# Taking the scale of tanh and exp from ScalarE registers in an attention loop

## The chip, the cores and the metric

The kernel runs on one core of a Trainium2 chip. The metric is the device time of one execution in microseconds (us). The kernel before was run three times; the median is 474.38 us (473.76 to 475.51). One further execution was profiled, and all rows below come from that one.

## The reference, cut to what matters

The program is an attention with soft-capped scores, followed by a mixture of experts in which every token goes to its best expert. In the attention there are 8 batches, 12 heads, 448 positions and a head size of 64, all in fp32:

```python
scale = 1.0 / np.sqrt(q.shape[-1])                      # 0.125
scores = scale * np.matmul(q, k.transpose(0, 1, 3, 2))
scores = cap * np.tanh(scores / cap)
scores = scores - np.max(scores, axis=-1, keepdims=True)
attn = np.exp(scores)
attn = attn / (np.sum(attn, axis=-1, keepdims=True) + 1e-09)
attn_out = np.matmul(attn, v)
...
expert_idx = np.argmax(x @ w_gate, axis=1)              # 3584 tokens, 8 experts, at most 80 kept in each
h = np.maximum(x[tok_idx] @ w1[e], 0.0)
out[tok_idx] = gate_w[tok_idx, None] * (h @ w2[e])
```

`cap` is an input of the program (30.0 here), so it is known only when the program runs.

## The kernel before

The attention is a loop over 24 units of work (`u`), each with four heads of one batch. A unit's score matrix is cut into 7 blocks of 128x896. For each block `scores` lets TensorE (PE) multiply q and k into a PSUM tile `sc`, of which there are two, and ScalarE (ACT) then writes `e = tanh(scl * sc)` to SBUF at line 1206, where `scl` is 0.125/cap. `expo` at line 1210 turns `e` in place into `exp(capt * e)`, in three pieces of 128x1792 (two blocks) and one of 128x896. So a unit has 7 tanh and 4 exp instructions, 11 in all, and the loop has 168 and 96. GpSimd (POOL) adds up parts of `e` for the row sums (lines 1216 and 1218), PE multiplies the `e` of the unit before with the values (`av`, lines 1237 and 1270) and with ones (`sp`), and VectorE (DVE) inverts the row sums (lines 1278 to 1283) and scales the result (`x`, line 1290).

The order of the instructions inside the loop is written out by hand in the string `STEPS`, under a manual schedule: `q` is a block of scores with its tanh, `e` an exp, `v` and `r` are passes of PE over the values of the unit before, `p` a sum on GpSimd, `s` and `n` the steps of VectorE. At the marks `b`, steps of the gate and of the routing of earlier batches are slipped in by a planner with estimated costs. Every engine runs its own instructions in that order. What stands ahead of the loop, from `scale()` on, is put in order by the scheduler of the kernel language, which goes by the order of the program and by what is ready.

`scl` and `capt` are SBUF columns of 128x1: `scale()` (lines 140 to 143) loads `cap` into `capt` by DMA, and VectorE makes `scl` of it. ScalarE reads one of these columns as the scale operand of each tanh and exp. In the first microseconds ScalarE's queue also issues two of the transfers of `load(0)` (line 1168): the lower halves of the first tiles of k and q. `guards()` (lines 195 to 203) has three small ACTIVATE instructions on `capt`, and one table load goes ahead of them.

After the loop the experts run from line 1609 on. Their weights are fetched by DMA at line 868 into a ring, of which eight buffers exist during the attention and ten more come from memory that the attention gives back at its end. At the very end, at line 1647, every engine loads one flag from SBUF into a register.

Of the kernel before, what the change touches and what calls it, by code (L numbers as in the profile page):

```python
# [9 lines left out]
I32 = mybir.dt.int32  # L10
AF = mybir.ActivationFunctionType
# [5 lines left out]
B, H, S, D = 8, 12, 448, 64  # L17
# [101 lines left out]
def attn_moe(ctx, tc, q2, k, v, cap, wg, w1, w2, capacity, ct, out):  # L119
    nc = tc.nc  # L120
# [11 lines left out]
    capt = consts.tile([128, 1], F32, name="capt")  # L132
    scl = consts.tile([128, 1], F32, name="scl")
# [6 lines left out]
    def scale():  # L140
        nc.sync.dma_start(capt, cap.broadcast_to([128, 1]))
        nc.vector.reciprocal(scl, capt)
        nc.vector.tensor_scalar(scl, scl, 0.125, None, op0=ALU.mult)
# [706 lines left out]
    wts, regs = [], {}  # L850
# [265 lines left out]
    st = {"laid": set(), "banks": ["misc"], "held": {}, "take": None, "read": 0, "late": False}  # L1116
# [29 lines left out]
    with ExitStack() as a2:  # L1146
# [8 lines left out]
        def load(u):  # L1155
            b, j = u // NQ, 2 * (u % NQ)
            qt = st["q", u] = qkp.tile([128, 2, S], F32, name=f"qt{u}", tag="qt")
            kt = st["k", u] = qkp.tile([128, 2, S], F32, name=f"kt{u}", tag="kt")
            parts = [(p, slice(0, 2), slice(0, S)) for p in (kt, qt)]
            if u == 0:  # L1160
                one, two, w0, w1 = slice(0, 1), slice(1, 2), slice(0, KR + CK), slice(KR + CK, S)
                parts = [(kt, one, w0), (qt, one, slice(0, S)), (kt, one, w1), (kt, two, slice(0, S)), (qt, two, slice(0, S))]
            for n, (p, x, y) in enumerate(parts):
                for h in range(2):
                    w = slice(64 * h, 64 * h + 64)
                    queue = nc.scalar if u == 0 and h == 1 and n < 2 else nc.sync
                    src = k[b, j + x.start:j + x.stop, :, h, y] if p is kt else q2[b, j + x.start:j + x.stop, w, h]
                    queue.dma_start(p[w, x, y], src.rearrange("j p s -> p j s"))
# [17 lines left out]
        def scores(u, x):  # L1186

            if ("e", u) not in st:
                st["e", u] = ep.tile([CK, 2 + 4 * NK, S], F32, name=f"e{u}", tag="e")
            ps = pss.tile([CK, 2, 512], F32, name=f"sc{u}_{x}", tag="sc")  # L1190
            if x == 0:
                for pr in range(2):
                    for m in range(4):
                        for h in range(2):
                            w = slice(64 * h, 64 * h + 64)
                            i, y = m // 2, NK * CK * (1 - h) + 32 * (m % 2)
                            nc.tensor.matmul(ps[32 * m:32 * m + 32, h, HQ * pr:HQ * pr + HQ], st["k", u][w, pr, y:y + 32], st["q", u][w, pr, HQ * i:HQ * i + HQ],
                                             start=True, stop=True)
            else:
                pr, c = divmod(x - 1, NK)  # L1200
                for m in range(4):
                    for h in range(2):
                        w = slice(64 * h, 64 * h + 64)
                        y = KR * h + c * CK + 32 * m
                        nc.tensor.matmul(ps[32 * m:32 * m + 32, h, :S], st["k", u][w, pr, y:y + 32], st["q", u][w, pr], start=True, stop=True)  # L1205
            nc.scalar.activation(st["e", u][:, 2 * x:2 * x + 2], ps[:, :, :S], AF.Tanh, scale=scl)  # L1206

        def expo(u, x0, x1):
            e = st["e", u][:, 2 * x0:2 * x1]
            nc.scalar.activation(e, e, AF.Exp, scale=capt)  # L1210

        def esum(u, pr, i):
            e = st["e", u][:, 2 + 2 * NK * pr:2 + 2 * NK * (pr + 1)]
# [261 lines left out]
        st["begun"] = 0  # L1475
        st["wait"] = lambda: (now.__setitem__(1, now[0]), ready_at.__setitem__(1, clock[1]))
        scale()
        load(0)
        ready = ps1.tile([128, 512], F32, name="ready", tag="sp")
        for _ in range(NSTART):  # L1480
# [21 lines left out]
        for w in range(NU + 1):  # L1502
# [13 lines left out]
            for i, x in enumerate(todo):  # L1516
                k_ = x[0]
                a_ = [int(y) for y in x[1:]]
                if k_ == 'q' and w < NU:
                    scores(w, TURNS[a_[0]])  # L1520
                elif k_ == 'q':
                    begin()
                elif k_ == 'e':
                    expo(w, *RUNS[a_[0]])
                elif k_ == 'p':
                    if w not in DIRECT:
# [166 lines left out]
```

## Time and profile before

| | us |
|---|---|
| median of three runs | 474.38 (473.76 to 475.51) |
| the profiled execution, its time | 474.13 |
| the profiled execution, its span | 472.3 |
| busy: PE / ACT / DVE / POOL | 437.2 / 331.9 / 244.4 / 239.7 |
| mean granted clock of TensorE | 0.986 of full speed |

The span runs from the first to the last instruction; 1.8 us of the execution lie outside it. A row of a group of instructions gives its line, engine, operation, the tiles written and read (out<-in), the shape, how often it occurs, its busy time, the mean of one in ns, and the idle time of the engine ahead of it with what ended it. The chain of work that ended last is followed back from the last instruction to what released it, or to the instruction before it on its engine. "PEld" is TensorE's loading of weights, "issue" is time in which the profile shows no wait. A queue's name with a q at its end (SPq, ACTq) stands for instructions that the engine's sequencer handles itself, such as the issue of a transfer or a load into a register.

### The profile page before, as it was taken

What the parts mean: (1) busy time and instruction counts of PE and PEld (TensorE: products, weight loads), DVE (VectorE), ACT (ScalarE), POOL (GpSimd) and SP (SyncE); (2) the same over time, 40 slices, a digit from 0 to 9 for tenths busy, and PEclk for the clock granted to TensorE, in tenths of its full rate; (3) what the DMA queues carried; (4) which work ended last, traced back from release to release, by engine and by line L of the source; (5) the groups of instructions that cost most, each with busy time, mean ns of one, the idle gap of its engine ahead of it and who ended that gap; (6) DMA issues with size and microseconds to landing.
All of it is one profiled execution on the core that took longest, in us unless ns stands there. A gap on an engine that the chain in (4) does not pass through costs nothing.

```text
span 472.3 us, 21423 instructions
## 1 busy us (share of the span) xinstructions
PE 437.2 (93%) x9533; PEld 224.0 (47%) x9533; DVE 244.4 (52%) x769; ACT 331.9 (70%) x349; POOL 239.7 (51%) x152
## 2 busy tenths in 40 slices
PE   7799989998999999899979999999799999999990
PEld 3344434444443444445434454443245667764670
DVE  2133355337535663775257856998537998510000
ACT  5999998998999899898969999979501221211210
POOL 1666655675765566665546755656425032372022
PEclk9999999999999999999989999999899999999997
DMA  6776694697679559745724672893727999999961
GB/s 159 162 193 196 181 281 131 177 266 195 197 191 265 141 162 267 200 145 157 213 63 130 177 198 79 244 232 104 237 71 270 399 333 327 338 393 408 398 256 30
DMA packets 68261, 101.10 MB, mean 214 GB/s; under 512 B 12448, under 2 KB 50608, under 8 KB 68160
## 3 DMA queue, kind: packets, MB, share of 16 engines
q1 hardware_dynamic: 66048, 96.23, 66.5%
q0 software_dynamic: 1920, 3.25, 2.1%
q8 instruction: 77, 1.26, 1.2%
q14 instruction: 24, 0.20, 0.1%
q10 hardware_dynamic: 192, 0.17, 0.1%
HBM read 76.11 MB, written 23.80 MB: 212 GB/s over the span
## 4 chain that ended last, share of the span: by engine, by line
PE 62%; ACT 14%; DVE 12%; DMA 6%; issue 4%; POOL 1%; SPq 0%; POOLq 0%; DVEq 0%
PE sc L1205 16%; PE av L1237 16%; PE hp L891 8%; ACT e L1206 8%; ACT e L1210 6%; DMA w<-in_w_dram 5%; PE yp L891 4%; PE sp L1237 3%; PE lgp L1316 2%; PE sp L1268 2%; DVE x L1290 2%; PE av L1270 2%; DVE w L319 2%; PE hp5a L891 1%; PE pd L447 1%
## 5 line engine op out<-in xcount | busy, mean ns | idle before, releaser
L1206 ACT ACTIVATE e<-sc,scl 128x896 f32<-128x896 f32 x168 | 164.1, 1002 | 21.2 <-PE sc L1205 21.1
L1237 PE MATMUL av<-e,vr 64*32 64x448 f32 x2304 | 163.4, 545 | 7.2 <-DVE x L1290 6.8
L1210 ACT ACTIVATE e<-e,capt 128x1792 f32<-128x1792 f32 (+1 forms) x96 | 153.5, 1599 | 0.8
L1205 PE MATMUL sc<-qt,kt 64*32 64x448 f32 x2304 | 141.2, 544 | 8.8 <-ACT e L1206 8.3
L1216 POOL TENSOR_TENSOR t<-e 128x896 f32<-128x896 f32 x46 | 96.9, 2107 | 90.6 <-ACT e L1210 90.1
L1218 POOL TENSOR_TENSOR t<-t,e 128x896 f32<-128x896 f32 x46 | 97.4, 2118 | 41.1 <-ACT e L1210 36.8
L1237 PEld LDWEIGHTS av<-e,vr 64*32 64x32 f32 x2304 | 53.4, 107 | 68.8 <-issue 42.2
L1205 PEld LDWEIGHTS sc<-qt,kt 64*32 64x32 f32 x2304 | 39.8, 106 | 56.5 <-issue 34.6
L1278 DVE STREAM_TRANSPOSE st<-sp 128x448 f32<-128x448 f32 x24 | 15.6, 650 | 91.0 <-PE sp L1237 84.8
L941 POOL DMA_INDIRECT out_dram<-ysv,si x18 | 18.6, 1035 | 61.2 <-ACT ysv L939 53.5
L1270 PE MATMUL av<-e,vr 64*32 64x224 f32 x384 | 46.5, 349 | 0.0
L891 PE MATMUL hp<-w,xt 128*32 128x256 f32 x720 | 42.4, 381 | 2.3 <-DVE xt L691 1.4
L1237 PE MATMUL sp<-t,ones 64*32 64x448 f32 x368 | 44.5, 543 | 0.0
L891 PE MATMUL yp<-w,thv 128*32 128x192 f32 x960 | 41.9, 327 | 0.6 <-DMA w<-in_w_dram 0.4
L1270 PE MATMUL av<-e,vx 64*32 64x224 f32 x384 | 41.7, 349 | 0.0
L1290 DVE TENSOR_TENSOR x<-av,r 128x448 f32<-128x448 f32 x48 | 27.7, 619 | 16.4 <-PE av L1237 16.3
L891 PEld LDWEIGHTS yp<-w,thv 128*32 128x32 f32 x960 | 30.1, 110 | 10.4 <-DMA w<-in_w_dram 2.4
L891 PEld LDWEIGHTS hp<-w,xt 128*32 128x32 f32 x720 | 21.9, 109 | 20.1 <-DMA w<-in_w_dram 3.4
L1270 PEld LDWEIGHTS av<-e,vr 64*32 64x32 f32 x384 | 22.6, 107 | 16.7 <-issue 15.9
L441 DVE TENSOR_SCALAR_CACHE_REDUCE gb<-krow,kc 112x896 bf16<-112x896 f32 (+7 forms) x36 | 30.0, 876 | 0.5 <-PE pd L447 0.5
L1268 PE MATMUL sp<-e,ones 64*32 64x224 f32 x384 | 27.9, 349 | 0.0
L1299 DVE STREAM_TRANSPOSE xb<-x 128x448 f32<-128x448 f32 x48 | 27.9, 619 | 0.0
(241 smaller groups left out, 417.4 us busy)
## 6 DMA issues: line engine op xcount, KB each, us to landing
w<-in_w_dram SPq DMA_DIRECT2D x36, 512.0 KB
w<-in_w_dram SPq DMA_DIRECT2D x48, 384.0 KB
vr<-in_v_dram SPq DMA_DIRECT2D x24, 512.0 KB
out_dram<-zero SPq DMA_DIRECT2D x14, 768.0 KB
xs<-xb SPq DMA_DIRECT2D x32, 336.0 KB
kt<-in_k_dram SPq DMA_DIRECT2D x46, 224.0 KB
qt<-in_q_dram SPq DMA_DIRECT2D x46, 224.0 KB
vx<-in_v_dram SPq DMA_DIRECT2D x48, 32.0 KB
```

The source lines that it names most:

```text
L441: nc.vector.tensor_scalar(g, krow[:, x:y], kp, 0.0, op0=ALU.is_ge, op1=ALU.add, accum_out=a)
L891: nc.tensor.matmul(spot(ps, g, q)[32 * j:32 * j + 32], of(g), w[:, q * j:q * j + q], start=(kk == 0 and g % 2 == 0), stop=(kk == last and ...
L1205: nc.tensor.matmul(ps[32 * m:32 * m + 32, h, :S], st["k", u][w, pr, y:y + 32], st["q", u][w, pr], start=True, stop=True)
L1206: nc.scalar.activation(st["e", u][:, 2 * x:2 * x + 2], ps[:, :, :S], AF.Tanh, scale=scl)
L1210: nc.scalar.activation(e, e, AF.Exp, scale=capt)
L1216: nc.gpsimd.tensor_tensor(t1, e[:, 0:2], e[:, 2:4], op=ALU.add)
L1218: nc.gpsimd.tensor_tensor(st["es", u, pr], st["es", u, pr], e[:, 4:6], op=ALU.add)
L1237: behind(nc.tensor.matmul(ps[32 * g:32 * g + 32, :S], v_, e, start=first, stop=final))
L1268: behind(nc.tensor.matmul(st["sp", u][32 * g:32 * g + 32, HQ * i:HQ * i + HQ], ones[w, 0:32], e, start=(part == 0), stop=False))
L1270: behind(nc.tensor.matmul(st["av", u, f][32 * g:32 * g + 32, HQ * i:HQ * i + HQ], last_of(u, pr, h, i)[w, 32 * f:32 * f + 32], e, start=Fa ...
L1290: nc.vector.tensor_tensor(st["x", u][:, f], st["av", u, f][:, :S], st["r", u], op=ALU.mult)
L1299: nc.vector.transpose(st["xt", b][:, :, j, :], st["x", u][:, f].rearrange("p (a b) -> p a b", b=32))
```

## The change

Two registers of ScalarE are allocated. Right after `scale()` and ahead of `load(0)` one is loaded from the first element of `scl` and the other from the first element of `capt`, as raw 32-bit values. Every tanh and exp of the loop names a register as its scale, in place of the 128x1 column. All rows of a column hold the same number, so the values are the same.

```diff
-            nc.scalar.activation(st["e", u][:, 2 * x:2 * x + 2], ps[:, :, :S], AF.Tanh, scale=scl)
+            nc.scalar.activation(st["e", u][:, 2 * x:2 * x + 2], ps[:, :, :S], AF.Tanh, scale=st["regs"][0])
...
-            nc.scalar.activation(e, e, AF.Exp, scale=capt)
+            nc.scalar.activation(e, e, AF.Exp, scale=st["regs"][1])
...
         scale()
+        st["regs"] = [nc.scalar.alloc_register(n) for n in ("sclr", "capr")]
+        for reg, t in zip(st["regs"], (scl, capt)):
+            nc.scalar.reg_load(reg, t[0:1, 0:1].bitcast(I32))
         load(0)
```

## Rows read from the trace of the kernel before

**Rows 1.** Busy time by stretch; columns: stretch, length, five engines, PEclk, DMA share, GB/s

```profile
17.00:45.00 28.00, 26.20 (x638) 12.11 (x624) 8.03 (x18) 27.90 (x27) 17.65 (x9) 1.00 0.62 171
...
236.00:256.00 20.00, 16.73 (x356) 7.40 (x355) 12.36 (x36) 16.05 (x17) 10.74 (x6) 0.91 0.41 108
...
440.00:450.00 10.00, 10.00 (x210) 6.99 (x206) 0.49 (x2) 2.04 (x6) 0.00 (x0) 1.00 1.03 396
```

**Rows 2.** Chain that ended last, in order of time: start us, us, what

```profile
17.25 0.90 ACT e L1206
...
44.01 1.00 ACT e L1206
...
75.69 1.01 ACT e L1206
...
281.04 0.99 ACT e L1206
```

**Rows 3.** Waits of PE and of its weight loads, 17 to 340 us; total, times, longest

```profile
PE sc L1205 <- ACT e L1206: 6.3, 9, 2.9
...
PEld sc L1205 <- ACT e L1206: 13.2, 19, 3.3
```

**Rows 4.** ScalarE's groups by line and shape: busy us, mean ns, idle before

```profile
L1206 ACT ACTIVATE e<-sc,scl 128x896 f32<-128x896 f32 x168 | 164.1, 1002 | 21.2 <-PE sc L1205 21.1
L1210 ACT ACTIVATE e<-e,capt 128x1792 f32<-128x1792 f32 x72 | 128.6, 1786 | 0.8
L1210 ACT ACTIVATE e<-e,capt 128x896 f32<-128x896 f32 x24 | 24.9, 1037 | 0.0
...
L907 ACT ACTIVATE hsv<-hp 128x768 f32<-128x768 f32 x5 | 4.1, 811 | 33.7 <-PE hp L891 33.7
...
L316 ACT ACTIVATE tau<-d 112x32 f32<-112x32 f32 x3 | 0.7, 228 | 0.9 <-DVE d L305 0.9
```

**Rows 5.** ScalarE's timeline, two stretches: start us, us, what

```profile
119.06 1.90 ACT L1206 ACTIVATE e<-sc,scl 128x896 f32<-128x896 f32 x2
120.84 1.79 ACT L1210 ACTIVATE e<-e,capt 128x1792 f32<-128x1792 f32 x1
122.52 1.02 ACT L1206 ACTIVATE e<-sc,scl 128x896 f32<-128x896 f32 x1
...
443.88 0.60 ACT L909 ACTIVATE hsv<-hp5a 128x512 f32<-128x512 f32 x1 [4.12 <-PE hp5a L891]
444.37 0.78 ACT L798 COPY gtv<-gq 32x3 f32<-32x3 f32 x4
```

**Rows 6.** Timeline of the first 17 us, all engines: start us, us, what, idle before

```profile
1.36 0.61 ACTq L1168 DMA_DIRECT2D qt<-in_q_dram  x1
...
3.47 0.18 ACT L199 ACTIVATE big<-capt 1x1 f32<-1x1 f32 x1
3.56 0.15 DVE L143 TENSOR_SCALAR scl<-scl 128x1 f32<-128x1 f32 x1
3.60 0.20 ACT L197 ACTIVATE guard<-guard 128x1 f32<-128x1 f32 x1
...
6.22 1.91 ACT L1206 ACTIVATE e<-sc,scl 128x896 f32<-128x896 f32 x2 [2.42 <-PE sc L1205]
...
16.33 0.98 PE L1197 MATMUL sc<-qt,kt 64*32 64x224 f32 x30 [0.29 <-DMA qt<-in_q_dram]
```

**Rows 7.** Instructions of three lines: count, duration ns min/median/max, first and last start

```profile
L868 SPq DMA_DIRECT2D w<-in_w_dram x84: 332/333/1742, 292.9 to 449.6; - x84
...
L1173 SPq DMA_DIRECT2D vr<-in_v_dram x24: 373/396/606, 10.5 to 330.1; - x24
...
L1647 ACTq TENSOR_LOAD <-fl_i x1: 475/475/475, 460.9 to 460.9; - x1
```

**Rows 8.** Timeline of VectorE and of GpSimd near 108 us

```profile
108.30 2.11 POOL L1218 TENSOR_TENSOR t<-t,e 128x896 f32<-128x896 f32 x1 [1.86 <-ACT e L1210]
...
108.64 1.82 DVE L319 TENSOR_TENSOR w<-tau,rd 112x32 f32<-112x32 f32 x1
```

## The prediction, made before the changed kernel was run

> **What bounds the kernel now.** I read the busy times by stretch first. In the early loop ScalarE is busy 27.90 of 28.00 us and PE 26.20 [rows 1]: two engines share the bound, and the question is which of them the end of the loop hangs on in which part. The chain that ended last answers that. Before 17.25 us it is ScalarE with waits on PE; from the tanh at 17.25 to the one at 44.01 it is nothing but ScalarE, 25 instructions one behind the other (16 tanh, 9 exp). Then PE takes it over. ScalarE comes back for short pieces only: 8 instructions from 75.69, 8 from 116.48, 1 at 239.34, 5 from 248.75 and 5 that end with the tanh at 281.04 [rows 2]. That makes 52 of the 264 tanh and exp; for the rest of the loop the chain runs through PE and, at the ends of some units, through VectorE. The waits of PE tell the same from the other side: from 17 to 340 us PE waited for a tanh 9 times, 6.3 us in all, the longest 2.9 us; its weight loads did so 19 times, 13.2 us, the longest 3.3 us [rows 3]. After the loop the expert weights fill the DMA (share 1.03) while ScalarE has 2.04 us of work in 10 [rows 1]; these loads need memory that the attention gives back, so the stage moves with the end of the loop and passes on what the loop gains.
>
> **What the column costs.** The change takes one operand from 168 tanh and 96 exp. Its price follows from comparing forms. The exp of 1792 columns takes 1786 ns and that of 896 takes 1037 [rows 4], so a column costs 749/896 = 0.836 ns. The ReLU at line 907 reads PSUM with a fixed scale: 811 ns at 768 columns, and 128 more would make it 918. The tanh, also out of PSUM, takes 1002: 84 ns more. Out of SBUF, the tanh at line 316 with its fixed scale of 0.5 takes 228 ns at 32 columns, which is 950 at 896, and the exp takes 1037: 87 ns more [rows 4]. I take 85 ns.
>
> That is a duration, and neighbours overlap, so the spacing has to show it too. Two tanh that start at 119.06 are followed by an exp at 120.84, 890 ns for each, 141 ns above their columns (749). A ReLU of 512 columns at 443.88 is followed by the next instruction after 490 ns, 62 ns above its columns (428) [rows 5]. The difference is 79 ns, so the overlap doesn't hide the column. ScalarE would have 264 x 0.085 = 22.4 us less to do, 0.94 us in each unit.
>
> The Trainium skill ("ScalarE: Activation LUTs", section "What ACT_TABLE_LOAD costs") gives about 93 ns for each 128x1 operand. The trace has 84 and 87. By the page's figure the 52 instructions would give 4.8 us. The page tells nothing of a scale in a register.
>
> **What a register costs in its place.** The trace has no ACTIVATE with a register, so I bound it. From below: as much as a fixed scale, saving the whole 85 ns; more than that has no reason. From above: the register is fetched only when the instruction's turn has come, and the overlap with the one ahead is lost; two tanh start 890 ns apart and last 1002, so that is 112 ns [rows 4, 5]. The nearest row of one operation with and without a register in its operands is SyncE's issue of a transfer of 128 partitions: 333 ns with an address from a register (line 868) and 396 with a fixed one (line 1173) [rows 7]. So a register there shows no surcharge. I take zero, and keep the surcharge of 112 ns for the range.
>
> **What the 85 ns are worth.** On the chain 52 x 0.085 = 4.4 us, and the chain sets a ceiling too: its PE and VectorE parts still have to be walked. From PE's side: of the 6.3 us the longest, 2.9 us, lies at 240 us, where ScalarE itself had been held up by VectorE, so 3.4 us are left [rows 3]. For the weight loads it is 13.2 - 3.3 = 9.9 us, of which some 0.22 us in each of 18 is the ordinary pause between bursts: 5.9 us. So the direct gain lies between 3.4 and 5.9 by PE's waits, with 4.4 as the chain's figure. I take 3.9, the middle of 3.4 and 4.4, as PE will become the later one within some of those pieces. The other 18 us or so of ScalarE's saving turn into longer waits for PE.
>
> **The start.** The eight instructions on the chain ahead of 17.25 would save 0.7 us, but PE waits at 16.33 us for the transfer of the second unit's q [rows 6], which no faster ScalarE brings in. I count nothing here.
>
> The two register loads cost about 475 ns each, by the one at line 1647 [rows 7]. They need `capt`, and `scl`, which is done at 3.56 + 0.15 = 3.71 us, and ScalarE then idles for 2.42 us until the first tanh at 6.22 [rows 6]. 0.95 us fits in: cost zero, with that idle time as the cover. Were the cover gone, 0.95 us would show, and most of it would be lost in the wait at 16.33 again. What is queued behind the two loads matters more. In the program they stand ahead of the two transfers that ScalarE's queue issues, the later at 1.36 us, and of `guards()`. The scheduler goes by what is ready: line 199 ran at 3.47 us ahead of line 197 at 3.60, which waits for line 196 [rows 6]. The transfers wait for nothing, so I expect them to stay in front.
>
> **The collisions.** A VectorE operation with two SBUF inputs waits until a running GpSimd sum is through: line 319 took 1.82 us at 108.64, and ended with the sum that began at 108.30, released by an exp [rows 8]. The chain crosses ten such places, this one among them. A tanh and an exp that are both shorter let the sum begin 0.17 us earlier, so the collision ends that much earlier: 0 to 1.7 us, less where PE holds the tanh. I take 0.4.
>
> **The sum.** 3.9 + 0.4 = 4.3 us. Against the profiled execution: 474.13 - 4.3 = 469.8 (472.3 of span and 1.8 outside it, which doesn't change). The median of the runs lies 0.25 us higher, so 470.1; I say 470.0.
>
> **The rivals.**
>
> - *The register is dear (slower).* If the sequencer fetches the value only at the instruction's turn, the 112 ns of overlap go, on top of a path that is no shorter than now. The place is the ScalarE-bound part of the loop. The least is 60 instructions of the chain (52 and the eight of the start) x 0.112 = 6.7 us, and with PE's slack used up at most 264 x 0.112 = 29.6 us. With ScalarE so near to its bound I take 10 us: 484. It decides as soon as the surcharge goes beyond the 85 ns saved. For it: nothing in the trace has such an operand. Against it: the address in a register shows no surcharge [rows 7]. By the Trainium skill ("Perfetto Trace Analysis", section "Per-engine timelines") an ACTIVATE is decoded and put into a wait queue ahead of its wait, which would read the register early; no row shows that for a register.
> - *The register costs as much as the column (the change doesn't do what it says).* Then nothing moves: 474.4.
> - *PE and the DMA keep the gain.* ScalarE gets its 85 ns, but PE's order and transfers such as the one at 16.33 us hold the early loop. Then 1 to 2 us come out: about 473. For it: PE is busy 26.20 of 28.00 us in the very stretch that is ScalarE's [rows 1].
> - *The register loads go first.* Then the transfers of ScalarE's queue wait for `scl` at 3.71 us and for two loads (0.95), and issue the later one at some 5.2 us in place of 1.36: 3.9 us late [rows 6, 7]. The first tanh moves by as much; against the wait at 16.33 about 3 us are left: 474.1 - 4.3 + 3.1 = 473.
> - *More than the chain says.* From 236 to 256 us PE's mean granted clock is 0.91 [rows 1], that is some 3.6 us at the lower level of 1.2 GHz, behind a stretch in which PE waited for VectorE. If an earlier GpSimd sum shortens that wait and the clock stays up, 1.7 us come on top, and with the collisions at their upper end it is 466.
>
> **How the numbers follow.** The forecast (gain of 2.4 to 6.5 us) has 0.50; more than that 0.07; PE and DMA keep it 0.13; the register loads first 0.06; no cheaper than the column 0.08; dear 0.16. A measurement of this kernel can tell about 0.5%, 2.4 us, from no change. So faster 0.57, within 0.27, slower 0.16. The forecast's own range is 467.5 to 472. For 8 in 10 the range takes in the cases without a gain and most of those with a larger one, and leaves out the dear register and a tail below: 466 to 476.
>
> **What would show it.** The tanh's mean should fall from 1002 to about 917 ns, the exps' from 1786 and 1037 to about 1700 and 950, and the spacing of two tanh from 890 to about 805. ScalarE's busy time falls by some 22 us; its idle time ahead of line 1206, 21.2 us now [rows 4], grows by some 18. The chain between 17 and 45 us should go over to PE in part, and the PE waits of rows 3 should shrink to about 3 us plus the place at 240. The first tanh should start at 6.2 us; a start near 10 us means that the transfers were held up. The prediction is wrong if the means stay or rise (the register's price), or if they fall as said and the time doesn't, in which case PE's order was the bound in the early loop too.

## The result: 1.2% slower, and the profile after

| | before | after |
|---|---|---|
| median of the comparison, us | 474.75 (473.76 to 475.51) | 480.44 (479.11 to 482.15) |
| profiled execution: time, span, us | 474.13, 472.3 | 480.97, 479.1 |
| end of the attention loop (end of its last exp), us | 340.5 | 347.5 |
| busy PE / ACT / DVE / POOL, us | 437.2 / 331.9 / 244.4 / 239.7 | 438.6 / 310.3 / 249.6 / 239.3 |

The ratio after to before is 1.0123, with a 95% interval of 1.0083 to 1.0163. The prediction was 470.0 us, in a range of 466 to 476: wrong in sign, and outside the range. The loop ends 6.9 us later and the span is 6.8 us longer, so the loss arises in the loop, and the experts pass it on.

ScalarE did get what the prediction promised it. Its groups by line and shape (busy us, mean ns, idle before) answer to [rows 4]; the column is gone from the names of the inputs:

```profile
L1206 ACT ACTIVATE e<-sc 128x896 f32<-128x896 f32 x168 | 150.7, 912 | 32.7 <-PE sc L1205 31.8
L1210 ACT ACTIVATE e<-e 128x1792 f32<-128x1792 f32 x72 | 121.9, 1693 | 0.8
L1210 ACT ACTIVATE e<-e 128x896 f32<-128x896 f32 x24 | 22.8, 952 | 0.0
```

The tanh is shorter by 90 ns, the exps by 93 and 85. ScalarE is busy 21.6 us less, and its idle time ahead of the tanh has grown by 11.5 us [rows 4], not by the 18 that were expected. Another 12.6 us came ahead of ScalarE's copies at line 423 (1.6 before, 14.2 after), which wait for PE in the four places shown below. The shares of the chain that ended last, on the page of after, say that it is no longer on the path (14% ACT and 62% PE before):

```profile
PE 76%; DVE 11%; DMA 4%; issue 4%; ACT 2%; POOL 1%; SPq 1%; POOLq 0%; DVEq 0%
```

The busy times by stretch, with the columns of [rows 1], tell where it went well and where not:

```profile
17.00:45.00 28.00, 27.55 (x664) 13.21 (x672) 8.03 (x18) 27.02 (x28) 18.87 (x10) 1.00 0.65 180
45.00:106.00 61.00, 57.98 (x1302) 27.30 (x1287) 26.98 (x83) 51.07 (x52) 35.54 (x17) 0.97 0.71 198
...
130.00:236.00 106.00, 99.56 (x2245) 47.26 (x2237) 58.86 (x163) 85.80 (x87) 61.58 (x30) 0.97 0.66 184
236.00:256.00 20.00, 17.58 (x406) 8.00 (x398) 9.42 (x25) 16.02 (x18) 10.55 (x6) 1.00 0.52 131
```

From 17 to 45 us PE is now busy 27.55 of 28 us (26.20 before): it has taken the stretch over. From 45 to 106 and from 130 to 236 its granted clock is 0.97 where it was 1.00 before, and PE is busy 1.5 and 3.4 us less. Before:

```profile
45.00:106.00 61.00, 59.49 (x1366) 27.38 (x1374) 25.46 (x84) 58.12 (x57) 38.82 (x19) 1.00 0.74 208
...
130.00:236.00 106.00, 103.00 (x2386) 48.40 (x2385) 57.32 (x168) 97.28 (x90) 62.89 (x30) 1.00 0.69 193
```

What ended PE's gaps stands in the waits of PE and of its weight loads from 17 to 345 us (total, times, longest):

```profile
PE av L1237 <- DVE x L1290: 15.5, 6, 3.2
PE sc L1205 <- ACT e L1206: 3.0, 2, 2.4
...
PEld av L1237 <- DVE x L1290: 27.7, 29, 4.0
...
PEld sc L1205 <- ACT e L1206: 7.7, 17, 2.8
```

The waits for a tanh went from 6.3 to 3.0 us and from 13.2 to 7.7, the way that was predicted [rows 3] and by a little more; 2.4 of the 3.0 us are one wait, at the place near 240 us (it ends at 248.99 here). But PE's wait for VectorE's `x` has more than doubled. Before it was this:

```profile
PE av L1237 <- DVE x L1290: 6.8, 7, 1.3
```

Now it is 15.5 us in 6 times: four of 3.02 us, one of 3.21 near the end of the loop, and a short one.

**The place.** I cut the loop by the 24 exps of 128x896, one for each unit, into 23 intervals (0 to 22; the expectations below call them units). Four of them, 5, 8, 11 and 14, lie behind the end of one of the first four batches, where VectorE has steps of the gate (lines 317 to 323) between the row sums and `x`. Interval 8 before:

```profile
112.57 1.04 ACT L1210 ACTIVATE e<-e,capt 128x896 f32<-128x896 f32 x1
...
127.05 1.04 ACT L1210 ACTIVATE e<-e,capt 128x896 f32<-128x896 f32 x1
```

and after:

```profile
113.87 0.95 ACT L1210 ACTIVATE e<-e 128x896 f32<-128x896 f32 x1
...
130.00 0.95 ACT L1210 ACTIVATE e<-e 128x896 f32<-128x896 f32 x1
```

That is 14.48 us against 16.13. Together the four went from 57.94 to 68.66 us, 10.7 us more. Interval 22 became 3.6 us longer (15.89 to 19.47), but from its end to the last exp the loop took 1.7 us less, so its end piece (interval 22 and what follows) is 1.9 us longer, 33.4 against 31.5. All the rest is 5.7 us shorter; the sum is the 6.9.

What happens there is seen when VectorE and GpSimd are read side by side. Before, the rows that follow [rows 8]:

```profile
110.71 0.16 DVE L322 TENSOR_SCALAR_CACHE_REDUCE us<-u 112x4 f32<-112x4 f32 x1
110.80 0.16 DVE L323 SCALAR_TENSOR_TENSOR kc<-u,wsc 112x4 f32<-112x4 f32 x1
110.87 1.15 DVE L1290 TENSOR_TENSOR x<-av,r 128x448 f32<-128x448 f32 x2
...
110.96 2.10 POOL L1216 TENSOR_TENSOR t<-e 128x896 f32<-128x896 f32 x1 [0.55 <-ACT e L1210]
```

The sum that holds line 319 ends at 108.30 + 2.11 = 110.41. Lines 320 and 322 follow, and `kc` at line 323, which has two SBUF inputs again, starts at 110.80, 0.39 us after the sum's end. GpSimd's pause is 0.55 us, so `kc` is 0.16 us ahead of the next sum and takes 0.16 us. The same place after:

```profile
109.97 2.12 POOL L1218 TENSOR_TENSOR t<-t,e 128x896 f32<-128x896 f32 x1 [1.85 <-ACT e L1210]
112.45 2.08 POOL L1216 TENSOR_TENSOR t<-e 128x896 f32<-128x896 f32 x1 [0.35 <-ACT e L1210]
...
110.49 1.65 DVE L319 TENSOR_TENSOR w<-tau,rd 112x32 f32<-112x32 f32 x1
...
112.40 0.16 DVE L322 TENSOR_SCALAR_CACHE_REDUCE us<-u 112x4 f32<-112x4 f32 x1
...
112.48 2.06 DVE L323 SCALAR_TENSOR_TENSOR kc<-u,wsc 112x4 f32<-112x4 f32 x1
114.47 1.14 DVE L1290 TENSOR_TENSOR x<-av,r 128x448 f32<-128x448 f32 x2
...
115.13 1.14 PE L1237 MATMUL av<-e,vr 64*32 64x448 f32 x9 [3.02 <-DVE x L1290]
```

The sums now start 2.48 us apart (2.66 before): between their releases lie a tanh and an exp, each some 90 ns shorter. The sum itself takes as long as ever, so all of that comes out of the pause: 0.36 us. `kc` still needs 0.39 us from the sum's end, starts 0.03 us after the next sum has begun, and takes 2.06 us, until that sum is through. `x` and with it PE, which has been idle for 3.02 us, wait for an operation on 112x4 numbers. The clock adds to the price. Interval 5, the same place one batch earlier, by stretch:

```profile
68.00:72.40 4.40, 1.38 (x31) 0.47 (x25) 4.33 (x9) 3.11 (x4) 3.97 (x3) 1.00 1.03 250
72.40:76.80 4.40, 4.40 (x66) 1.69 (x58) 2.15 (x15) 1.09 (x2) 0.58 (x1) 0.61 0.05 11
```

PE is busy 1.38 of 4.40 us while it waits, and the next 4.40 us are granted 0.61: most of that time is at the lower level of 1.2 GHz. Sixteen matmuls of line 1205 take 0.96 us before the gap and 1.75 in the low-clock stretch behind it:

```profile
67.44 0.96 PE L1205 MATMUL sc<-qt,kt 64*32 64x448 f32 x16
71.42 1.14 PE L1237 MATMUL av<-e,vr 64*32 64x448 f32 x9 [3.02 <-DVE x L1290]
...
74.39 1.75 PE L1205 MATMUL sc<-qt,kt 64*32 64x448 f32 x16
```

### The profile page after: what moved, and what is told of

It is laid out like the page before. It is cut to its first block, busy times and chain, and to the rows that moved or that the text cites. A ratio compares the mean times of both kernels' runs of the same rounds, so it can differ in the third digit from the quotient of the medians.

```text
span 479.1 us, 21424 instructions
## 1 busy us (share of the span) xinstructions
PE 438.6 (92%) x9533; PEld 229.9 (48%) x9533; DVE 249.6 (52%) x769; ACT 310.3 (65%) x349; POOL 239.3 (50%) x152
## 4 chain that ended last, share of the span: by engine, by line
PE 76%; DVE 11%; DMA 4%; issue 4%; ACT 2%; POOL 1%; SPq 1%; POOLq 0%; DVEq 0%
PE av L1237 21%; PE sc L1205 20%; PE hp L891 9%; PE yp L891 7%; PE sp L1237 3%; PE av L1270 3%; PE sp L1268 3%; PE lgp L1316 2%; PE sc L1197 2%; DVE x L1290 2%; DMA w<-in_w_dram 1%; PE pd L447 1%; PE hp5a L891 1%; DMA vr<-in_v_dram 1%; ACT e L1206 1%
## 5 line engine op out<-in xcount | busy, mean ns | idle before, releaser
L1237 PE MATMUL av<-e,vr 64*32 64x448 f32 x2304 | 166.7, 547 | 16.5 <-DVE x L1290 16.3
L1206 ACT ACTIVATE e<-sc 128x896 f32<-128x896 f32 x168 | 150.7, 912 | 32.7 <-PE sc L1205 31.8
L1205 PE MATMUL sc<-qt,kt 64*32 64x448 f32 x2304 | 143.2, 542 | 5.1 <-ACT e L1206 4.4
L1210 ACT ACTIVATE e<-e 128x1792 f32<-128x1792 f32 (+1 forms) x96 | 144.7, 1508 | 0.8
L1237 PEld LDWEIGHTS av<-e,vr 64*32 64x32 f32 x2304 | 54.1, 107 | 77.8 <-issue 41.5
L1205 PEld LDWEIGHTS sc<-qt,kt 64*32 64x32 f32 x2304 | 41.4, 106 | 50.5 <-issue 35.1
L1270 PE MATMUL av<-e,vr 64*32 64x224 f32 x384 | 49.2, 357 | 0.0
L1270 PE MATMUL av<-e,vx 64*32 64x224 f32 x384 | 43.6, 357 | 0.0
L891 PEld LDWEIGHTS hp<-w,xt 128*32 128x32 f32 x720 | 23.6, 110 | 17.7 <-issue 3.3
L1270 PEld LDWEIGHTS av<-e,vr 64*32 64x32 f32 x384 | 23.6, 109 | 16.4 <-issue 16.0
L1268 PE MATMUL sp<-e,ones 64*32 64x224 f32 x384 | 29.8, 366 | 0.0
```

The lines of the kernel that those rows point to most:

```text
L891: nc.tensor.matmul(spot(ps, g, q)[32 * j:32 * j + 32], of(g), w[:, q * j:q * j + q], start=(kk == 0 and g % 2 == 0), stop=(kk == last and ...
L1210: nc.scalar.activation(e, e, AF.Exp, scale=st["regs"][1])
L1237: behind(nc.tensor.matmul(ps[32 * g:32 * g + 32, :S], v_, e, start=first, stop=final))
L1268: behind(nc.tensor.matmul(st["sp", u][32 * g:32 * g + 32, HQ * i:HQ * i + HQ], ones[w, 0:32], e, start=(part == 0), stop=False))
L1270: behind(nc.tensor.matmul(st["av", u, f][32 * g:32 * g + 32, HQ * i:HQ * i + HQ], last_of(u, pr, h, i)[w, 32 * f:32 * f + 32], e, start=Fa ...
```

## The experiments

The theory: the registers do what was predicted, and `kc` falling on the next GpSimd sum costs more than they bring. The rivals: the registers, or a clock that falls as ScalarE leaves PE's path, cost the time wherever `kc` stands; or what VectorE does there is of no account, since PE's own order binds. Each kernel was compared with the kernel before on the same chip; two of the chips need some 26 us more for the experts, with the kernel before too (its medians there are 501.5 and 501.7 us), so times are compared as ratios. These two chips (one with e1_kc_late, e2, e3 and e4, the other with e6_key_late_again and e8) also have an end piece of 32.9 to 33.8 us where before has 31.5; e2, which is before but for one moved operation, reaches interval 22 at the same time as before to 0.2 us and ends its loop 1.6 us later. So intervals can be set beside those of other chips, and loop ends only within some 2 us. "Four intervals" are 5, 8, 11 and 14; all lengths are us.

| kernel | ratio to before, 95% | loop end | four intervals | interval 22 | end piece |
|---|---|---|---|---|---|
| before | 1 | 340.5 | 14.48 14.48 14.49 14.49 | 15.89 | 31.5 |
| after | 1.0123 (1.0083 to 1.0163) | 347.5 | 17.71 16.12 17.52 17.31 | 19.47 | 33.4 |
| e0_after_again | 1.0171 (1.0111 to 1.0230) | 350.9 | 17.71 16.12 17.36 17.25 | 19.80 | 33.9 |
| e1_kc_late | 0.9962 (0.9927 to 0.9996) | 335.6 | 14.14 14.15 14.14 14.15 | 15.86 | 33.8 |
| e1_kc_late_again | 0.9842 (0.9791 to 0.9893) | 338.2 | 14.14 14.15 14.14 14.15 | 19.77 | 33.9 |
| e2_kc_late_columns | 0.9994 (0.9972 to 1.0016) | 342.1 | 14.42 14.41 14.42 14.42 | 15.98 | 33.2 |
| e3_tanh_only | 0.9959 (0.9922 to 0.9995) | 338.3 | 14.30 14.31 14.30 14.30 | 16.23 | 33.5 |
| e4_exp_only | 0.9965 (0.9932 to 0.9998) | 339.2 | 14.30 14.31 14.30 14.31 | 16.20 | 33.3 |
| e5_nudge | 0.9944 (0.9909 to 0.9979) | 337.3 | 14.24 14.24 14.24 14.24 | 19.63 | 33.9 |
| e6_key_late | 0.9873 (0.9813 to 0.9933) | 331.6 | 13.78 13.78 13.78 13.78 | 15.81 | 29.9 |
| e6_key_late_again | 0.9900 (0.9860 to 0.9939) | 334.0 | 13.78 13.78 13.78 13.78 | 15.67 | 32.9 |
| e8_key_late_columns | 0.9966 (0.9939 to 0.9993) | 339.4 | 14.23 14.23 14.23 14.22 | 15.96 | 33.1 |

**e0_after_again: the changed kernel once more,** beside e1_kc_late_again, e5_nudge and e6_key_late on one chip.

> The changed kernel once more, to stand beside the others on one chip. Collision theory: the loop's last exp ends near 347 us again, `kc` takes 2.06 us in four units, ratio about 1.012 on a chip whose expert stage passes the loop's time on. If the loop ends before 342 us, the loss seen first was an accident of one execution.

It is slower again, by 1.7%, with the four intervals the same to 0.2 us. The loop ends at 350.9 us, not near 347: interval 17 took 14.26 us in place of 12.56, and 1.4 us were lost before interval 5. The sum and `kc` stand as before to a few hundredths, though the loop runs 1.4 us later here:

```profile
113.89 2.08 POOL L1216 TENSOR_TENSOR t<-e 128x896 f32<-128x896 f32 x1 [0.35 <-ACT e L1210]
...
113.93 2.06 DVE L323 SCALAR_TENSOR_TENSOR kc<-u,wsc 112x4 f32<-112x4 f32 x1
```

So this place isn't left to chance: a sum's end starts VectorE's chain, and ScalarE's pace starts the next sum.

**e1_kc_late and e2_kc_late_columns: `kc` out of the way.** Line 323 is put behind the two scalings `x` for the first four batches, with registers (e1) and with columns (e2). `put_off` keeps the instruction back until both scalings are issued.

```diff
-            nc.vector.scalar_tensor_tensor(kcb, u, 2.0 ** -28, wsc, op0=ALU.max, op1=ALU.mult)
+            put_off(lambda: nc.vector.scalar_tensor_tensor(kcb, u, 2.0 ** -28, wsc, op0=ALU.max, op1=ALU.mult))
...
                     scaled(w - 1, a_[0])
+                    if a_[0] == 1:
+                        for f in st.pop("defer", None) or ():
+                            f()
```

> The changed kernel, with one VectorE operation moved: the key `kc` (line 323) of batches 0 to 3 runs after the two scalings `x` (line 1290) of its unit, not ahead of them. Theory (collision): the shorter exp lets GpSimd's next sum begin 0.03 us ahead of `kc`, which then takes 2.06 us in place of 0.16 and holds `x`, PE's next pass, and the clock behind it. With `kc` out of the way the four long units (17.71, 16.12, 17.52 and 17.31 us) go back to 14.5 us or less, `x` no longer waits, and the time is 468 to 472 us. Rival 1 (the register form slows the loop by itself): still 479 to 481. Rival 2 (a denser ScalarE and PE pull the granted clock down): still 478 or more, with as many stretches at the lower clock level as in the changed kernel (4 up to the end of the loop, 2 before).

> The kernel before (scales from 128x1 columns) with the same move of `kc`. Theory (collision): here `kc` took 0.16 us, there is nothing to win, so 474 to 475.5 us. If the move is worth something by itself, whatever the registers do (a rival reading of the run before), this falls as much as the run with registers does, to 470 or less.

One instruction of 112x4 numbers, moved past two others, takes 12.1 us out of the four intervals (68.66 to 56.58). In e1 (lines counted six higher by the edit):

```profile
108.36 2.09 POOL L1222 TENSOR_TENSOR t<-e 128x896 f32<-128x896 f32 x1 [0.35 <-ACT e L1216]
...
108.40 1.15 DVE L1296 TENSOR_TENSOR x<-av,r 128x448 f32<-128x448 f32 x2
109.46 1.01 DVE L329 SCALAR_TENSOR_TENSOR kc<-u,wsc 112x4 f32<-112x4 f32 x1
```

`x` reads PSUM and one SBUF input and runs at its normal pace beside the sum; `kc` still waits for that sum, 1.01 us, but PE doesn't wait for it. With columns the same move changes nothing measurable (0.9994), since `kc` had got in ahead anyway. The granted clock of e1 is 1.00 from 45 to 256 us, and PE's wait for `x` is back to what it was before:

```profile
PE av L1243 <- DVE x L1296: 6.0, 7, 1.0
```

The rival that the registers, or a clock that falls because ScalarE leaves PE's path, cost the time by themselves falls: e1 has the same registers, ScalarE has 2% of its chain as in after, and the clock stays up. I split the 12.1 us thus: interval 8, which had no low-clock stretch behind it, lost 1.97 us against e1, about the 1.90 that `kc` grew; the other three lost 3.57, 3.38 and 3.16, so I put 1.2 to 1.6 of each down to the clock.

> The changed kernel with `kc` behind the scalings, repeated beside the changed kernel itself. Collision theory: the loop ends near 335.6 us, some 12 us ahead of the changed kernel: 4 x 1.9 us of `kc` and three stretches of 3.4 us at the lower clock level that no longer occur (1.7 us each at most). Rival (the register form or the clock by itself): no more than 3 us between the two.

Beside the changed kernel on the same chip, 466.86 to 471.92 against 480.30 to 485.20 us, and the loop ends 12.7 us earlier, near the 12 expected (though at 338.2 us, not 335.6). The four intervals are as in e1, interval 22 is not; that is taken up below.

**e3_tanh_only and e4_exp_only: half of the change.** A register for the tanh alone, or for the exp alone, and the column for the other.

```diff
-            nc.scalar.activation(e, e, AF.Exp, scale=st["regs"][1])
+            nc.scalar.activation(e, e, AF.Exp, scale=capt)
```

> The changed kernel with a register for the tanh alone; the exp reads its column again. Theory (collision): between two of GpSimd's sums lay 0.55 us before and 0.35 after, and VectorE needs some 0.39 to get `kc` in. A tanh and an exp each take 0.09 of that, so with one of them 0.46 is left, `kc` takes 0.16 us, and the time is 470 to 474 us: each half alone is no slower than the kernel before, only both are. Rival 1 (the register form costs by itself, in proportion): about 478.

> The changed kernel with a register for the exp alone; the tanh reads its column again. Theory (collision): as for the tanh alone, 0.46 us between the sums, `kc` at 0.16 us, 470 to 474 us. Rival 1: about 477. If the two halves add up to what both do, the collision is not what decides.

Each half is a gain, of 0.4% (only just clear of the noise), and the loop ends 2.2 and 1.4 us earlier than before, in spite of the longer end piece of that chip; both together lose 6.9. Here the pause is shortened once, to 0.45 and 0.44 us, and `kc` still gets in, 0.06 and 0.05 us ahead. e3:

```profile
108.81 0.16 DVE L323 SCALAR_TENSOR_TENSOR kc<-u,wsc 112x4 f32<-112x4 f32 x1
...
108.87 2.10 POOL L1216 TENSOR_TENSOR t<-e 128x896 f32<-128x896 f32 x1 [0.45 <-ACT e L1210]
```

and e4:

```profile
109.92 0.16 DVE L323 SCALAR_TENSOR_TENSOR kc<-u,wsc 112x4 f32<-112x4 f32 x1
...
109.97 2.10 POOL L1216 TENSOR_TENSOR t<-e 128x896 f32<-128x896 f32 x1 [0.44 <-ACT e L1210]
```

The pauses are 0.55, 0.45, 0.44 and 0.36 us, and the need 0.39: three kernels pass and one doesn't, and that one is the slow one.

**e5_nudge: the sum held back instead.** Nothing of VectorE is moved. GpSimd gets a copy of 32 columns, whose result the sum overwrites, ahead of the sum of each unit's second pair of heads.

```diff
+                if pr == 1:
+                    nc.gpsimd.tensor_copy(t1[:, 0, 0:32], e[:, 2, 0:32])
```

> The changed kernel with work added: GpSimd copies 32 columns of `e` right ahead of the first sum of each unit's second pair (line 1216), so that this sum begins some 0.1 to 0.2 us later; nothing of VectorE, ScalarE or PE is changed. Collision theory: the pause between two sums grows from 0.35 us to more than the 0.39 that VectorE needs, `kc` gets in at 0.16 us, and the loop ends at 335 to 338 us, 9 to 12 us ahead of the changed kernel although more work is done. Rival 1 and rival 2 (register form, clock): no faster than the changed kernel, 347 us or later.

More work makes the kernel faster: 472.78 us against 484.36 for the changed kernel without it, and 0.56% below before. The sum starts after `kc`:

```profile
108.44 0.21 POOL L1217 COPY t<-e 128x32 f32<-128x32 f32 x1 [0.34 <-ACT e L1210]
108.72 2.10 POOL L1218 TENSOR_TENSOR t<-e 128x896 f32<-128x896 f32 x1
...
108.48 0.18 DVE L323 SCALAR_TENSOR_TENSOR kc<-u,wsc 112x4 f32<-112x4 f32 x1
```

**e6_key_late and e8_key_late_columns: the whole of lines 317 to 323 behind `x`.** With registers (e6) and with columns (e8). This takes the collision of line 319 off PE's path as well.

```diff
+            if usb is not None and st.get("defer") is not None:
+                st["defer"].append(rest)
+            else:
+                rest()
```

`rest` holds lines 317 to 323.

> The changed kernel with the whole VectorE part of the key (lines 317 to 323) of batches 0 to 3 behind the two scalings of its unit, so that the collision of line 319 (1.65 us in four units, 1.82 before) leaves the path to `x` as well. Collision theory: the four units fall from 14.1 us with `kc` alone late by up to 1.7 us each, the loop ends at 329 to 333 us, and the time falls to 0.97 to 0.985 of the kernel before where the expert stage passes it on. If PE's order has become the bound, the four units stay at 13.8 us or more.

> The kernel before (columns as scale), with VectorE's lines 317 to 323 put behind the two scalings at line 1290 for batches 0 to 3, as in e6_key_late. Theory (the registers bring what the chain and PE's waits say, 3.4 to 5.9 us, once nothing of VectorE meets a GpSimd sum on the path): units 5, 8, 11 and 14 fall from 14.48 to about 13.8 us, 2.7 us in all, so the loop ends near 337.8 us and the time is about 472; e6_key_late stays 4 to 6 us ahead of it. Rival (the move did it all and the registers are worth nothing by themselves, PE's order being the bound): the loop ends at 332 us and the time is 467 to 468, as e6_key_late's.

> The same kernel as e6_key_late (registers, VectorE's lines 317 to 323 behind the scalings), once more, beside e8_key_late_columns on one chip. Theory: loop end near 331.6 us, or 335 where the last slow unit (22) is the long one, and 467 to 471 us; 4 to 6 us ahead of e8_key_late_columns. Rival: level with it.

e6 beats both kernels: 467.46 us, 1.3% below before, and 1.0% on the second chip. Its loop ends at 331.6 us, within the range expected; the time, 0.987 of before, fell a little less than expected (0.97 to 0.985). Alone in a pause, line 319 (317 in this kernel's numbering) takes 0.19 us, in place of 1.82 [rows 8]:

```profile
107.64 0.19 DVE L317 TENSOR_TENSOR w<-tau,rd 112x32 f32<-112x32 f32 x1
```

Yet with columns the four intervals fall only from 14.48 to 14.23, where I had expected 13.8, and the loop ends at 339.4 in place of 337.8. PE's waits show why: `kc` still falls on a sum, the next one (1.63 us long in e6, 2.00 in e8), and the gate's own matmul now waits for it, in e8 longer than in e6. First e6, then e8:

```profile
PE psk L428 <- DVE kc L321: 5.2, 4, 1.3
```

```profile
PE psk L428 <- DVE kc L321: 6.6, 4, 1.7
```

So taking the first collision away as well was worth 0.19 us in each interval with columns (14.42 in e2, 14.23 in e8) and 0.36 with registers (14.14 in e1, 13.78 in e6), not the 1.82 and 1.65 us that it lasts: the path goes over to another wait. On one chip e6 ends the loop 5.4 us ahead of e8 (334.0 against 339.4) and is 3.3 us faster (496.03 against 499.34; the experts' stage varies by some us there). That is what the registers bring where nothing of the key stands ahead of `x`; a part of it, in the four intervals, lies in the shorter wait for `kc` in e6.

## Why the prediction was wrong, point by point

- *The column's price, 85 ns: right.* Measured 90, 93 and 85. ScalarE's saving, 22.4 us by the sum, was 21.6. The Trainium skill's figure ("ScalarE: Activation LUTs", section "What ACT_TABLE_LOAD costs"), about 93 ns, is at the upper end of the three.
- *The register costs nothing: right.* Two tanh that took 1.89 to 1.91 us together now take 1.71 to 1.73 where they follow at once. With that the dear register (10 us) and the register as dear as a column both fall.
- *The start costs nothing: right, though not in the order that I gave.* The transfers stayed in front. The load of `scl` ran ahead of the first tanh, that of `capt` behind the first two. The two loads after (count, duration ns min/median/max, first and last start):

```profile
L1480 ACTq TENSOR_LOAD <-scl x1: 473/473/473, 4.1 to 4.1; - x1
L1480 ACTq TENSOR_LOAD <-capt x1: 287/287/287, 8.3 to 8.3; - x1
```

  Both were covered: the first tanh starts at 6.27 us (6.22 before), the first exp at 9.14 (9.28 before).
- *The direct gain of 3.9 us: right in size.* Outside the four intervals and the end piece, after is 5.7 us shorter than before; 2.2 of that are interval 17 (next point), which varies, and 3.5 are left. Taken the same way, the other profiles of kernels with both registers have 2.1 (e0) to 4.0 (e5). e6 against e8 on one chip gives 5.4 us of loop, 1.8 of it in the four intervals. The bounds given were 3.4 and 5.9. That PE would soon be the later one was right too: intervals 1 and 2 fell from 12.47 and 12.42 to 12.22 and 11.88, some 0.2 and 0.5 us, where ScalarE has 0.94 us less to do; 11.87 is the shortest from interval 1 on that any kernel here shows.
- *The clock near 240 us.* In after's profile the stretch 236 to 256 stands at 1.00 (0.91 before) and interval 17 is 12.56 us in place of 14.72. The rival "more than the chain says" came true there, in this one execution: in e0 the same stretch is at 0.91 again, and the interval 14.26. The lower level came instead where I had not looked, behind the gaps of intervals 5, 11 and 14 and of the one near the end of the loop.
- *The collisions, a gain of 0.4 us: this is the step that failed.* It said: "A tanh and an exp that are both shorter let the sum begin 0.17 us earlier, so the collision ends that much earlier". The 0.17 us was right, and so was its first consequence: line 319 takes 1.65 us in place of 1.82. But I followed only the collision that was in the trace. The same 0.17 us brings the next sum forward as well, and the pause between two sums, 0.55 us before, becomes 0.38 by that sum (measured 0.36). In that pause VectorE had to get from the sum's end to the start of `kc`, 0.39 us by rows of before that I had at hand. It was a margin of 0.16 us against a shift of 0.17. The term, +0.4 us, measured about -11 us in the four intervals (10.7 against before, 12.1 against e1).
- *The rivals.* The one that ended slower, with a chance of 0.16, had the wrong mechanism, and nothing among the cases stood for a VectorE step that falls behind the next sum. So the range had no reason to reach beyond 476. At the other end, the terms of "more than the chain says" come to 474.1 - 3.9 - 1.7 - 1.7 = 466.8 us, not 466.
- *The last sign of being wrong.* It said that shorter instructions without a shorter time would mean that PE's order was the bound in the early loop too. The means fell and the time rose, and that reading would have misled: PE did take the early loop over, but the time was lost in its waits for `x`.

That such an operation waits at all was no surprise. The prediction said so by [rows 8]. The Trainium skill ("SBUF — State Buffer", section "Who interferes with whom") puts it as a rule: a VectorE instruction with two SBUF inputs contends with a GpSimd instruction that reads SBUF, for a pair of ports that is locked to one of them at a time, and the order of issue decides which of the two is blocked. The traces agree: `kc` takes 0.16 us when it is 0.05 us ahead and 2.06 when it is 0.03 us behind, and `x`, with one SBUF input, runs beside a sum at its usual pace, 1.15 us for two. What was missing was to apply it to the instruction that had only just escaped.

**What stays open: the end of the loop.** Interval 22 is 15.7 to 16.2 us in eight of the profiles and 19.5 to 19.8 in the other four, for one and the same program in e1_kc_late and e1_kc_late_again. In after, a sum starts while line 636 is at work, with two SBUF inputs of VectorE again, ahead of the row sums of that unit:

```profile
309.88 2.93 DVE L636 TENSOR_TENSOR prlh<-r,ctt 112x384 bf16<-112x384 f32 x2
...
310.16 2.23 POOL L1218 TENSOR_TENSOR t<-t,e 128x896 f32<-128x896 f32 x1 [1.31 <-ACT e L1210]
```

Before, both operations have begun when the next sum starts, and take 1.02 us:

```profile
303.87 1.02 DVE L636 TENSOR_TENSOR prlh<-r,ctt 112x384 bf16<-112x384 f32 x2
...
304.77 2.11 POOL L1218 TENSOR_TENSOR t<-t,e 128x896 f32<-128x896 f32 x1 [1.52 <-ACT e L1210]
```

The other profiles go the same way: the two operations take 2.93 to 2.94 us in all four with a long interval 22 and 1.02 in all eight with a short one, and only the four have a stretch at the lower clock level inside interval 22. It looks like the same collision with the same price, but no run moved `prlh` alone, so that is argued and not shown. The loss is not the whole 3.6 us either. All six profiles with a short interval 22 and an end piece of 32.9 to 33.8 us come from the two chips with the longer expert stage. On the other chips the end piece is 33.4 to 33.9 us with a long interval 22 and 31.5 (before) or 29.9 (e6_key_late, at a granted clock of 1.00 there, before and after at 0.95) with a short one. What decides which of the two a run gets I can't say; between before and after it is 1.9 of the 6.9 us.

## What to carry to other kernels

When an engine becomes faster, don't only ask which waits get shorter: list what now starts earlier, and for each small operation that slips through a gap between two long ones, set its margin against the shift. Here a margin of 0.16 us, all of it in rows of before, decided about 11 us. An operation of VectorE with two SBUF inputs that PE waits for should not stand between two GpSimd sums; moved behind what PE needs, it costs less here, and only then was the faster engine worth about what its path said.

## What the runs showed of the hardware that I had not expected

- A delay of 1.9 us on VectorE became 3.2 to 3.6 us in three of four places, because PE's granted clock fell to the lower level, 1.2 GHz, behind the gap (a mean of 0.61 from 72.40 to 76.80 us, after PE had been busy 1.38 of 4.40 us).
- A tiny operation waits as long as a larger one: `kc` with 112x4 numbers took 2.06 us and line 319 with 112x32 took 1.65, each until the sum beside it was through; alone they take 0.16 and 0.19.
- The phase between the sums and VectorE's chain is nearly the same in both profiles of the changed kernel (`kc` starts 0.02 to 0.04 us behind the sum in all eight places). A margin of 0.05 to 0.06 us (e4) held in all four intervals.
